# One queue, eight positions: reordering the transfers of steps 15 to 17 in a fused attention and MLP kernel

## The chip, the cores and the metric

The kernel runs on one core of one Trainium2 chip. The metric is the device time of one execution in microseconds; a figure for a kernel is the median over several executions. The profile is that of one execution, and its times count from the start of the profiled span.

## The reference

Two layers follow each other. The first is a decayed linear attention over 4 batches, 8 heads, 768 positions and 64 channels per head, in blocks of 64 positions with a state carried from block to block:

```
for each block b of 64 positions:
    intra = ((qb @ kb^T) * Dmask) @ vb
    inter = (qb * lam_pow) @ kv_state
    out   = intra + inter
    kv_state = lam_block * kv_state + (kb * rev_pow)^T @ vb
```

The second takes the attention output as a 3072 x 512 matrix x and computes `gelu_tanh(x @ w_in) @ w_out`, with an inner width of 2048. All inputs and the output are float32; the matmuls run in float16 with float32 sums.

## The kernel before

**Steps and groups.** The attention is cut into 24 steps, numbered 0 to 23. A step is 256 positions of one batch for four of the eight heads. Two steps make a superblock of 256 rows of x; the superblocks are put together into seven groups (line 533: `[[0, 1], [2], [3], [4, 5], [6, 7], [8, 9], [10, 11]]`), and each group runs the second layer on its rows. The matmuls of a group are cut into pieces that are put into a list, `filler`; `fill(n)` takes n pieces from it. So TensorE alternates between short bursts of attention and long runs of second-layer matmuls.

**The order of the work is written out by hand.** Every instruction is issued through `pin`, which keeps it in program order on its engine. Lines 913 to 1111 are the schedule. Nothing reorders it. What an engine waits for is decided by the data and by the rotation of buffers.

**One step, from load to score.** For step s the queries, keys and values are loaded by `load_step` (line 70) into float32 tiles of 256 KB each, which rotate over four buffers for each name. `cast_q` (line 282, on VectorE) multiplies the queries by their decay, `cast_k` (line 295, on ScalarE) converts the keys, both into one float16 tile. From step 8 on, `transpose_dma` (line 303) sends that tile through a transposing DMA into `qkT`, which rotates over five buffers. `scale_v` (line 266, on GpSimd) multiplies the values by the inverse decay.

**A burst.** Steps 13 to 16 and 18 to 23 are done two at a time by `burst(ns, ss)` (line 415): first `scores` of both steps in `ns` (line 350, into the PSUM tiles S), then, for the steps `ss` of the burst before, the products with the values (line 436) and with the carried state (line 461) into O, and the new state products K (line 450). In between the call may issue `ahead`, which for the burst of 15 and 16 is the preparation of step 17. Behind the matmuls come the masks of the scores on VectorE (line 360, `PT`), the copies of O into x on ScalarE (line 487), and the state updates (line 506 on VectorE, line 513 on GpSimd). A burst takes all eight PSUM banks: four S, two O, two K. The next second-layer matmul (line 560, `Hps`) goes into the bank of the first S, and so it waits until line 360 has read that one.

**The queue that the change is about.** All loads but two, all transposing DMAs and all stores are issued by SyncE, one after the other in program order. SyncE waits for what a transfer needs before it issues it, and whatever stands behind it waits too. The stores of a one-superblock group are issued by `store` inside `product` (line 662) at the moment when the piece that makes their data is taken from `filler`; for the third group (g = 2, rows 768 to 1023) there are two stores of 256 KB, one filled by VectorE at line 674 and one by ScalarE at line 656 and GpSimd at line 683.

**The order on that queue around the change.** The loop of steps 8 to 12 ends with n = 12, at lines 1032 to 1046. Written out, SyncE issues: transposition of 14; values of 15; values of 16; the two stores of the third group; transposition of 15; transposition of 16 (`prep_qk(16)`, line 1051); queries, keys, values of 17 (line 1052); queries, keys, values of 18 (line 1059); transposition of 17.

The lines of the schedule that matter:

```
1032        elif n == 12:
1033            load_step(15, "v")
1034            load_step(16, "v")
...
1044        if n == 12:
1045            prep_qk(15)
...
1051    prep_qk(16)
1052    load_ahead(17)
...
1055    burst((13, 14), (12,))
...
1061    burst((15, 16), (13, 14), ahead=lambda: (prep_qk(17), scale_v(17)))
```

Of the kernel before, what the change touches and what calls it, by code (L numbers as in the profile page):

```python
# [15 lines left out]
def kernel(  # L16
# [10 lines left out]
    nc = tc.nc  # L27
    pin = tc.keep_in_program_order
# [31 lines left out]
    def load_step(s, names="qkv"):  # L60
        b, r = divmod(s, 2 * NSB)
        sb, half = divmod(r, 2)
        ts = ld32.setdefault(s, [])
        for nm, src in (("q", q), ("k", k), ("v", v)):
            if nm not in names:
                continue
            t = ld.tile([P, HH, 2, D], FP32, tag=nm + "32", name=f"{nm}32_{s}")
            rows = src[b, half * HH : (half + 1) * HH, sb * SB : (sb + 1) * SB, :]
            queue = nc.scalar if (nm, s) == ("v", 0) else nc.sync
            pin(queue.dma_start(out=t[:].rearrange("p h j d -> p h (j d)"),  # L70
                                in_=rows.rearrange("h (p j) d -> p h (j d)", j=2)))
            ts.append(t)
# [97 lines left out]
    def load_ahead(s):  # L170
        if s < NSTEP:
            load_step(s)
# [76 lines left out]
    def wide(t):  # L249
        return t.rearrange("p j h d -> p h j d")  # L250

    def decay(t, s):
        hs = halves[s % 2]
        return t[:, hs, :].unsqueeze(3).to_broadcast([P, HH, 2, D])
# [9 lines left out]
    def scale_v(s):  # L264
        tv = a16p.tile([P, 2, HH, D], FP16, tag="v16", name=f"v16_{s}")
        pin(nc.gpsimd.tensor_tensor(wide(tv[:]), ld32[s][2][:], decay(dv, s), ALU.mult))  # L266
        a16[s] = a16[s] + (tv,)

    def prep_qk(s):
        cast_qk(s)  # L270
        transpose_dma(s)

    def cast_qk(s):
        cast_q(s)
        cast_k(s)

    def cast_q(s):
        q32 = ld32[s][0]
        tqk = a16p.tile([P, 2, 2, HH, D], FP16, tag="qk16", name=f"qk16_{s}")
        tq, tk = tqk[:, 0], tqk[:, 1]  # L280
        q_eng = nc.gpsimd if s == 3 else nc.vector
        pin(q_eng.tensor_tensor(wide(tq), q32[:], decay(dq, s), ALU.mult))  # L282
        if s == 0:
            inverse(halves[0])
            odd(halves[1])
            inverse(halves[1])
        a16[s] = (tq, tk)
        whole_qk[s] = tqk

    def cast_k(s):  # L290
        tk, k32 = a16[s][1], ld32[s][1]
        if s == 4:
            pin(nc.vector.tensor_copy(out=wide(tk), in_=k32[:]))
        else:
            pin(nc.scalar.activation(out=wide(tk), in_=k32[:], func=AF.Copy))  # L295
# [3 lines left out]
    def transpose_dma(s):  # L299
        tqk = whole_qk.pop(s)  # L300
        if s >= FIRST_DMA_T:
            o = qkp.tile([P, 2, 2, 2, P], FP16, tag="qkT", name=f"qkT_{s}")
            pin(nc.sync.dma_start_transpose(out=o[:].rearrange("p a j h t -> p (a j h) t"),
                                            in_=tqk[:].rearrange("p a j h d -> p (a j h d)")))
            qkT[s] = o
            if s == FIRST_DMA_T + 1:
                load_step(s + 1, "v")
# [225 lines left out]
    groups = [[0, 1], [2], [3], [4, 5], [6, 7], [8, 9], [10, 11]]  # L533
    group_of = {sb: (g, i) for g, sbs in enumerate(groups) for i, sb in enumerate(sbs)}
    filler = []
    o_pairs = {}

    def store_pair(pair):
# [4 lines left out]
    def queue_group(g, lead=0, per_set=0):  # L543
# [71 lines left out]
        def product(m, p, part=None):  # L615

            st = of_group

            def bank(name):
                if name not in st:  # L620
                    st[name] = ps_M.tile([P, 1 if name == "X" else NP, HE], FP32, tag="M",
                                         name="M" + name[0])
                return st[name]

            if m in (2, 5, 3):
                dst = bank("Y" if m in (5, 3) else "W")[:, p]
            else:
                dst = bank(f"X{p}")[:, 0]
            opens = m == 1 or (m in (2, 5) and p == 0)
            closes = m in (2, 3, 4)  # L630
            a, b = FACTORS[m]
            for i in range(HF) if part is None else range(HF // 2 * part, HF // 2 * part + HF // 2):
                lhsT = g_rows(a, i)[:, p * P : p * P + P]
                if b in W_SUMS:
                    rhs = w_sum16[:, w_slot[b], i, :]
                else:
                    F, E = b
                    rhs = w_out16[:, F * HF + i, E * HE : E * HE + HE]
                pin(nc.tensor.matmul(dst, lhsT, rhs, start=(opens and i == 0),  # L639
                                     stop=(closes and i == HF - 1), skip_group_check=True))  # L640
            if part == 0:
                return
            last = p == NP - 1

            def temp(name):
                if name not in st:
                    st[name] = mtp.tile([P, NP, HE], FP32, tag=name, name=name)
                return st[name]

            def out_tile(T):  # L650
                if f"o{T}" not in st:
                    st[f"o{T}"] = otp.tile([P, NP, 2, HE], FP32, tag="o32", name=f"o{T}")
                return st[f"o{T}"]

            def copy(to, of):
                pin(nc.scalar.activation(out=to, in_=of, func=AF.Copy))  # L656

            def store(T, ps=slice(0, NP), es=slice(0, 2)):
                r = row0 + T * HN
                rows = out[r : r + HN, :].rearrange("(p q) (e d) -> q p e d", q=P, e=2)  # L660
                for i in [slice(i, i + 1) for i in range(ps.start, ps.stop)]:
                    pin(nc.sync.dma_start(out=rows[:, i, es], in_=out_tile(T)[:, i, es, :]))

            one = slice(p, p + 1)
            if m == 1:
                copy(temp("m1")[:, p], dst)
            elif m == 2 and last:
                pin(nc.vector.tensor_tensor(out_tile(0)[:, :, 0, :], st["W"][:], st["m1"][:], ALU.add))
            elif m == 5 and last:
                copy(temp("q")[:], st["Y"][:])  # L670
            elif m == 6:
                copy(temp("u2")[:, p], dst)
            elif m == 3 and last:
                pin(nc.vector.tensor_tensor(out_tile(0)[:, :, 1, :], st["Y"][:], st["u2"][:], ALU.add))
                store(0)
            elif m == 7 and last_group:
                pin(nc.vector.tensor_tensor(out_tile(1)[:, p, 1, :], dst, st["q"][:, p], ALU.add))
                if last:
                    store(1, one, slice(1, 2))
            elif m == 7:  # L680
                copy(temp("u3")[:, p], dst)
                if last:
                    pin(nc.gpsimd.tensor_tensor(out_tile(1)[:, :, 1, :], st["u3"][:], st["q"][:],  # L683
                                                ALU.add))
            elif m == 4:
                copy(out_tile(1)[:, p, 0, :], dst)
                if last_group:
                    store(1, one, slice(0, 1 if last else 2))
                elif last:
                    store(1)  # L690
# [218 lines left out]
    def U(n):  # L909
        update(n, 1)  # L910
# [98 lines left out]
    for n, (a, b, c, d) in FILL.items():  # L1009
        stage_t(n)  # L1010
        fill(a + (n == 10))
        if n == 8:
            cast_q(n + 2)
            fill(1)
            cast_k(n + 2)
            transpose_dma(n + 2)
        else:
            prep_qk(n + 2)
        if n < 11:
            load_step(n + 4, "qkv" if n < 10 else "qk")  # L1020
        if n == 9:
            store_pair(1)
        if n == 11:
            scale_v(13)
            load_step(14, "v")
            load_step(16, "qk")
        elif n == 9:
            scale_v(11)
        elif n == 10:
            scale_v(12)  # L1030
            load_step(15, "qk")
        elif n == 12:
            load_step(15, "v")
            load_step(16, "v")
            scale_v(14)
        fill(b + (n == 8) - (n == 10))
        R(n, n - 1, keep=n == 8)
        fill(c)
        if n == 8:
            update(n, 0)  # L1040
            scale_v(n + 2)
            fill(2)
        U(n)
        if n == 12:
            prep_qk(15)
            scale_v(15)
        fill(d)
        if n > 8:
            sum_win((n - 7) // 2, (n - 1) % 2, nc.vector)

    prep_qk(16)
    load_ahead(17)
    scale_v(16)
    fill(3)
    burst((13, 14), (12,))
# [84 lines left out]
```

## Time and profile before

| what | value |
|---|---|
| device time, median of three executions | 200.13 us (199.81 to 200.23) |
| the profiled execution | 200.43 us, of which the span is 198.5 us |
| TensorE clock granted over the span | full |
| TensorE matmuls busy | 191.1 us, 96% of the span |
| VectorE busy | 152.5 us, 77% |
| ScalarE busy | 121.9 us, 61% |
| GpSimd busy | 73.0 us, 37% |
| moved by DMA | 38.13 MB, of which 37.50 MB on SyncE's queue |

How to read it. An engine's busy share says how much of the span it worked, not whether its idle time matters. For that one looks at the waits of the engine that sets the end, at the chain of work that ended last, and at the timeline of the stretch concerned. For a transfer two times count: when SyncE issued it, and when it landed. An issue row of the timeline shows only the first; from issue to landing a 256 KB load took 5.0 to 5.3 us in the middle of the page's issue table, and a store 4.6 us. A row such as `DMA_TRANSPOSE ... x2` merges two neighbours into one.

### The profile page before, as it was taken

The page shows a single profiled execution, that of the slowest core. Times are in us where ns is not written, and L with a number is a line of the kernel's source. Part 1 is how long each engine was busy: PE and PEld are TensorE (multiplying, and loading weights), DVE is VectorE, ACT ScalarE, POOL GpSimd, SP SyncE. Part 2 cuts the span into 40 slices and gives each one's busy share as a digit, 9 for nine tenths or more (in the row PEclk, how much of TensorE's full clock was granted, in tenths as well). Part 3 has the DMA queues.
Part 4 walks back from the last instruction along what each step waited for, and adds up shares of the span by engine and source line. Part 5 has one row for each costly group of instructions (what it writes and reads, how often), then busy time and mean ns, then how long its engine had stood idle before and what let it go on. Part 6 is the DMA issues. An engine that isn't in the chain of part 4 may idle for free.

```text
span 198.5 us, 5914 instructions
## 1 busy us (share of the span) xinstructions
PE 191.1 (96%) x2431; PEld 139.8 (70%) x2431; DVE 152.5 (77%) x297; ACT 121.9 (61%) x249; POOL 73.0 (37%) x85
## 2 busy tenths in 40 slices
PE   8979999999999999999799999999999999999993
PEld 2546544556888888654488855578888888888882
DVE  4897722889999889757899957998778996588620
ACT  3673878367874685677645377854768836779321
POOL 6594213466455831196372626256002030002000
PEclk9999999999999999999999999999999999999999
DMA  6999999999999999998995999410211300020205
GB/s 172 291 326 386 385 386 386 290 292 284 242 222 246 258 325 239 214 293 216 216 276 127 235 338 201 108 23 0 53 58 51 107 7 0 0 109 0 106 15 200
DMA packets 62810, 38.13 MB, mean 192 GB/s; under 512 B 18624, under 2 KB 55744, under 8 KB 62784
## 3 DMA queue, kind: packets, MB, share of 16 engines
q1 hardware_dynamic: 62240, 37.50, 73.5%
q8 instruction: 19, 0.31, 0.7%
q10 hardware_dynamic: 544, 0.26, 0.5%
q14 instruction: 7, 0.06, 0.1%
HBM read 27.26 MB, written 6.29 MB: 169 GB/s over the span
## 4 chain that ended last, share of the span: by engine, by line
PE 85%; DMA 7%; SPq 4%; ACT 1%; DVE 1%; issue 0%
PE Hps L560 22%; PE MX L639 18%; PE MY L639 9%; PE HX L730 7%; PE O2ps L575 7%; PE MW L639 4%; DMA wi<-in_moe_w_in_dram 4%; SPq L70 4%; PE HY L730 4%; PE S L350 3%; PE Hps L821 3%; DMA q<-in_q_dram 2%; PE HW L730 2%; PE OK L408 2%; PE OK L399 1%; PE O L461 1%
## 5 line engine op out<-in xcount | busy, mean ns | idle before, releaser
L560 PE MATMUL Hps<-xT,w_in 128*128 128x512 f16 (+1 forms) x288 | 50.5, 332 | 1.1 <-DVE PT L360 1.1
L513 POOL TENSOR_TENSOR u<-t,lumask 128x256 f16<-128x256 f32 x40 | 30.4, 776 | 41.6 <-DVE t L506 26.5
L560 PEld LDWEIGHTS <-w_in 128*128 128x128 f16 x288 | 27.9, 98 | 20.3 <-issue 1.3
L564 ACT ACTIVATE gT<-Hps 128x512 f16<-128x512 f32 x56 | 33.4, 598 | 11.6 <-PE Hps L560 11.1
L360 DVE TENSOR_TENSOR PT<-S,mask 128x512 f16<-128x512 f32 x48 | 30.3, 681 | 6.5 <-PE S L350 6.5
L266 POOL TENSOR_TENSOR v<-v,dv 128x512 f16<-128x512 f32 x24 | 27.9, 1165 | 18.2 <-DMA v<-in_v_dram 17.8
L639 PEld LDWEIGHTS <-gs 128*128 128x128 f16 x320 | 31.2, 98 | 3.6
L639 PEld LDWEIGHTS <-gT 128*128 128x128 f16 x240 | 23.3, 98 | 3.2 <-ACT gT L564 0.2
L282 DVE TENSOR_TENSOR qk<-q,dq 128x512 f16<-128x512 f32 x23 | 19.5, 851 | 3.2 <-DMA q<-in_q_dram 3.1
L639 PE MATMUL MX<-w_sum,gs 128*128 128x256 f16 x160 | 21.4, 273 | 0.0
L295 ACT ACTIVATE qk<-k 128x512 f16<-128x512 f32 x23 | 14.4, 625 | 9.5 <-DMA k<-in_k_dram 9.2
L683 POOL TENSOR_TENSOR o<-u,q 128x512 f32<-128x512 f32 (+1 forms) x5 | 6.0, 1205 | 34.9 <-ACT u L656 34.9
L609 DVE TENSOR_TENSOR gs<-gT 128x1024 f16<-128x1024 f16 (+1 forms) x24 | 16.0, 671 | 1.6 <-ACT gT L564 1.6
L575 PE MATMUL O2ps<-w_out,gT 128*128 128x512 f16 x64 | 14.6, 379 | 0.0
L487 ACT ACTIVATE xT<-OK 128x256 f16<-128x256 f32 x26 | 9.9, 452 | 6.5 <-PE OK L408 6.2
L730 PEld LDWEIGHTS <-ws 128*128 128x128 f16 x128 | 12.5, 97 | 1.8
L656 ACT ACTIVATE u<-MX 128x256 f32<-128x256 f32 x18 | 6.9, 383 | 10.2 <-PE MX L639 10.2
L609 DVE TENSOR_TENSOR gs<-gT,gs 128x1024 f16<-128x1024 f16 (+1 forms) x12 | 10.8, 901 | 0.3
L487 ACT ACTIVATE xT<-O 128x256 f16<-128x256 f32 x22 | 8.0, 459 | 4.9 <-PE O L461 4.0
L350 PEld LDWEIGHTS <-qkT 64*64 64x64 f16 x384 | 6.0, 106 | 6.8 <-issue 3.2
L575 PEld LDWEIGHTS <-gT 128*128 128x128 f16 x64 | 6.1, 98 | 6.6
L639 PE MATMUL MY<-w_out,gs 128*128 128x256 f16 x80 | 10.7, 272 | 0.0
(96 smaller groups left out, 316.7 us busy)
## 6 DMA issues: line engine op xcount, KB each, us to landing
q<-in_q_dram SPq DMA_DIRECT2D x24, 256.0 KB, 5.0
k<-in_k_dram SPq DMA_DIRECT2D x24, 256.0 KB, 5.1
v<-in_v_dram SPq DMA_DIRECT2D x23, 256.0 KB, 5.3
out_dram<-o SPq DMA_DIRECT2D x23, 256.0 KB, 4.6
wo<-in_moe_w_out_dram SPq DMA_DIRECT2D x4, 1024.0 KB, 9.5
wi<-in_moe_w_in_dram SPq DMA_DIRECT2D x4, 512.0 KB, 8.2
wi<-in_moe_w_in_dram SPq DMA_DIRECT2D x2, 1024.0 KB, 12.8
v<-in_v_dram ACTq DMA_DIRECT2D x1, 256.0 KB, 4.3
```

What stands on the lines that cost most here:

```text
L266: pin(nc.gpsimd.tensor_tensor(wide(tv[:]), ld32[s][2][:], decay(dv, s), ALU.mult))
L282: pin(q_eng.tensor_tensor(wide(tq), q32[:], decay(dq, s), ALU.mult))
L295: pin(nc.scalar.activation(out=wide(tk), in_=k32[:], func=AF.Copy))
L360: pin(nc.vector.tensor_tensor(t[:, hl].rearrange("p b c d -> p b (c d)"), Sps[:].rearrange("p b c d -> p b (c d)"), mask[:].unsqueeze(1).t ...
L487: pin(nc.scalar.activation(out=d, in_=o, func=AF.Copy))
L513: pin(nc.gpsimd.tensor_tensor(u[:], state[half][:].unsqueeze(2).to_broadcast([P, 2, 2, D]), lumask[:, 2 * half : 2 * half + 2, :].unsqueez ...
L560: pin(nc.tensor.matmul(by_block(Hps[:, i, :]), w_in16[:, c, f * P : (f + 1) * P], x(c), start=(c == 0), stop=(c == NC - 1)))
L564: pin(nc.scalar.activation(out=dst, in_=Hps[:], func=AF.Gelu_apprx_tanh))
L575: pin(nc.tensor.matmul(O2[tau][0][:], gT[:, f % HF, f // HF, tau * P : (tau + 1) * P], w_out16[:, f, :], start=(n == 0), stop=(n == NF - 1)))
L609: pin(nc.vector.tensor_tensor(g_rows(m, i), g_rows(a, i), g_rows(b, i), op))
L639: pin(nc.tensor.matmul(dst, lhsT, rhs, start=(opens and i == 0), stop=(closes and i == HF - 1), skip_group_check=True))
L730: pin(nc.tensor.matmul(dst[:, i, :], w_in_block(a, slice(c, c + 1), slice(f * P, f * P + P))[:, 0], x_block(b, slice(c, c + 1))[:, 0], sta ...
```

## The change

Three moves on SyncE's queue, and nothing else: no instruction is added or taken away, and the order on the four compute engines is that of before.

1. The transposition of 15 stands right behind that of 14. The loads of the values of 15 and 16 move behind it.
2. The queries and keys of 17 stand ahead of the transposition of 16; the values of 17 stay behind it. To that end `prep_qk(16)` is written out as its two halves, the casts and the transposition.
3. The two stores of the third group are kept in a list, `kept_stores`, when their data is made, and are issued behind the values of 17.

The aim is that transfers which a later step waits for are not held up on the queue by those that nobody waits for. The new order is: transpositions of 14 and 15; values of 15; values of 16; queries and keys of 17; transposition of 16; values of 17; the two stores; queries, keys, values of 18; transposition of 17.

```
+    kept_stores = []
...
             def store(T, ps=slice(0, NP), es=slice(0, 2)):
                 r = row0 + T * HN
                 rows = out[r : r + HN, :].rearrange("(p q) (e d) -> q p e d", q=P, e=2)
-                for i in [slice(i, i + 1) for i in range(ps.start, ps.stop)]:
-                    pin(nc.sync.dma_start(out=rows[:, i, es], in_=out_tile(T)[:, i, es, :]))
+                o = out_tile(T)
+
+                def send():
+                    for i in [slice(i, i + 1) for i in range(ps.start, ps.stop)]:
+                        pin(nc.sync.dma_start(out=rows[:, i, es], in_=o[:, i, es, :]))
+
+                if g == 2:
+                    kept_stores.append(send)
+                else:
+                    send()
...
         elif n == 12:
-            load_step(15, "v")
-            load_step(16, "v")
             scale_v(14)
...
         if n == 12:
             prep_qk(15)
+            load_step(15, "v")
+            load_step(16, "v")
             scale_v(15)
...
-    prep_qk(16)
-    load_ahead(17)
+    cast_qk(16)
+    load_step(17, "qk")
+    transpose_dma(16)
+    load_step(17, "v")
+    while kept_stores:
+        kept_stores.pop(0)()
     scale_v(16)
```

## Prediction

> **What bounds the kernel now.** I read the page first, then TensorE's waits, then the chain of work that ended last, then the timelines of the stretch that these point to. Part 1 of the page, with busy us, share of the span and number of instructions:
>
> ```profile
> PE 191.1 (96%) x2431; PEld 139.8 (70%) x2431; DVE 152.5 (77%) x297; ACT 121.9 (61%) x249; POOL 73.0 (37%) x85
> ```
>
> TensorE is busy for 96% of the span, so only what makes it idle can change the end. Its waits between 40 us and 198 us, as us in total, times, longest:
>
> ```profile
> PE Hps L560 <- DVE PT L360: 1.1, 1, 1.1
> ```
>
> That is one single wait in 158 us. TensorE's own timeline around it shows where it lies:
>
> ```profile
> 93.68 0.64 PE L350 MATMUL S<-qkT 64*64 64x128 f16 x32
> ...
> 94.95 0.51 PE L461 MATMUL O<-qkT,u 128*128 128x128 f16 x6
> 96.59 1.67 PE L560 MATMUL Hps<-xT,w_in 128*128 128x512 f16 x7 [1.13 <-DVE PT L360]
> ```
>
> The burst of steps 15 and 16 begins at 93.68 and ends at 94.95 + 0.51 = 95.46; then TensorE stands still for 1.13 us until 96.59. The chain of work that ended last says why (start, us, what):
>
> ```profile
> 90.08 0.19 SPq L303
> 90.26 0.05 issue
> 90.32 4.91 DMA q<-in_q_dram
> 95.22 0.02 issue
> 95.25 0.69 DVE qk L282
> 95.94 0.61 DVE PT L360
> 96.55 0.04 issue
> 96.59 3.61 PE Hps L560 x16
> ```
>
> Read upward: the matmul waits for a bank that the first mask (line 360) must have read; the mask stands behind the query cast of step 17 (line 282) on VectorE; the cast waits until the queries of 17 have landed at 95.22; they were issued at 90.32, as soon as SyncE was through with a transposition. SyncE's timeline tells what held it up:
>
> ```profile
> 81.47 1.72 SPq L303 DMA_TRANSPOSE qkT<-qk  x1
> 83.24 1.13 SPq L70 DMA_DIRECT2D v<-in_v_dram  x2
> 84.47 1.78 SPq L662 DMA_DIRECT2D out_dram<-o  x2
> 86.42 3.84 SPq L303 DMA_TRANSPOSE qkT<-qk  x2
> 90.32 0.57 SPq L70 DMA_DIRECT2D q<-in_q_dram  x1
> ```
>
> In order: transposition of 14, values of 15 and 16, two stores, transpositions of 15 and 16, queries of 17. The stores take 1.78 us because the second starts only at 85.90, when GpSimd has finished its output tile at 85.87. The cast tile of 15 was complete at 83.23 (VectorE 82.55 + 0.68, ScalarE 82.36 + 0.62), so its transposition stood ready for 3.2 us behind others.
>
> [...] the wait of the second store to 85.87 holds the transposition of 15 until 86.42. [...] Here the queries of 17 had arrived on 12 of 16 engines by 93.49, and on the last at 95.22. [...] the scores of 15 began at 93.68, yet their mask began at 95.86, behind the cast. [...] So I use landing times for arrivals.
>
> **The change part by part.** The counts and orders on the four compute engines stay; only SyncE's order moves. What SyncE will do, from 83.19 on, when it has issued the transposition of 14:
>
> *Transposition of 15 forward.* Ready at 83.23. An issue takes, over the 16 of before, as ns min/median/max and as us to landing:
>
> ```profile
> L303 SPq DMA_TRANSPOSE qkT<-qk x16: 1233/1510/3418, 50.7 to 141.0; - x16
> DMA to landing us min/median/max: 3.0/4.6/6.4
> ```
>
> I take 1.8 (it stands right behind another, whose data moves only from about 84.4 to 85.4), so it is issued by 85.0; the ends are 84.5 and 86.7. It lands near 87.5 instead of 91.40. Nobody gains from that by itself: its scores begin at 93.68.
>
> *Values of 15 and 16 back by one transposition.* Issued at 85.0 and 85.6 instead of 83.24 and 83.92, landing at 88 to 89.5 and 89 to 90.5 instead of 86.87 and 87.82 (3.6 and 3.9 us of before, up to 5). GpSimd's two multiplications (1.05 us each) then end by about 91.6, at worst 92.6, instead of 89.08. Queued behind them on GpSimd are the four state tiles of line 513, 0.61, 0.61, 1.06, 1.06 us. The burst at 93.68 reads the values at about 94.55 and the first two of the state tiles at 94.95; they are there by 92.8, at worst 93.8. Cost: nothing, hidden behind TensorE's second-layer matmuls.
>
> *Queries and keys of 17 forward.* Issued at about 86.1 and 86.7 instead of 90.32 and 90.93. At 4.9 us to landing the queries arrive at 91.0; the ends are 89.3 (3.2 us, the quickest load of this stretch, at 98.15) and 93.0 (6.9 us, the queries of 15). VectorE is free at 93.13, so the cast runs from 93.13 to 93.82 without a wait. In the burst before, the first mask began 0.46 us after the scores (87.62 against 87.16); so here at 94.14, ending at 94.83. The bank is free at about 94.88, and TensorE needs it at 95.46. The wait of 1.13 us goes away whole, with 0.6 us to spare. The keys land by 93.5 at worst; ScalarE casts them behind the gelu that ends at 94.39, ahead of the first copy of O at about 95.2.
>
> *Transposition of 16 behind three more transfers.* Its tile is complete at 85.79. It is issued at about 87.3 instead of 88.95 and lands 4.6 us later at 91.9, at most 6.4 later at 93.7, instead of 92.22. TensorE needs it about 0.28 us into the burst, at 93.96. On the expected path nothing is lost, but this is the thinnest margin of the change.
>
> *Values of 17 and the stores.* The values go out near 89.5 (91.51 before), and are multiplied on GpSimd after the state tiles, for a step that begins at 104.5. The stores go out near 90 instead of 84.47; the output pool has three buffers, and the buffer that waits for the first of these stores is written next at 112.6. Cost nothing. The loads of 18 follow at about 91 (92.06 before), the transposition of 17 no later than before.
>
> *Sum:* 1.13 us from TensorE's path, nothing added. Behind 96.59 TensorE has no wait over 0.06 us to the end, so the shift carries through if the others keep up. VectorE, busy without pause from 95.25 to 115.80, starts that stretch 1.7 us earlier (first mask 94.14 instead of 95.86), more than TensorE's 1.13. 200.13 - 1.13 = 199.0.
>
> **The rivals.** *Only a part is gained.* The profiled execution took 200.43 us, the others 199.81 to 200.23; if the wait is shorter without the profile, the gain is too. And if a transposition stalls the DMA engines, as from 88.75 to 90.25, where they moved 60 GB/s against 347 before and 265 after, the transposition of 16 comes up to 1.5 us later than 91.9 plus some lag, 94.5, and TensorE waits 0.5 there. Gain about 0.6: 199.5.
>
> *The wait is not there in undisturbed executions.* For: a single DMA engine brought the queries 1.7 us after the 12 others, and with 93.49 as landing there would have been no wait. Against: the keys and values of 17 and 18 trail alike, so it is no chance of one packet. Then 200.1.
>
> *Slower: the transposition of 16 becomes the bound.* With the longest issue (3.4 us) for that of 15, SyncE reaches that of 16 at 88.9; 6.4 us to landing is 95.3, and a stall of 1.5 us on top 96.8. The burst's remaining 1.5 us of matmuls follows, so the next second-layer matmul begins at 96.8 to 98.3 instead of 96.59: 0.2 to 1.7 us lost, 200.9 in the middle. For: that longest issue stood beside an equally full queue at 76.12. Against: two more transfers stood ahead then, and total data ahead of the transposition of 16 is what it was, two stores traded for two loads.
>
> **How the numbers follow.** Full gain 0.64 (199.0), part 0.14 (199.5), none 0.10 (200.1), slower 0.12 (200.9). The predicted time is the likeliest, 199.0. The range from 198.6 (the scatter of 0.4 below) to 200.3 holds the first three cases and a little of the last. Faster by over 0.2%, that is below 199.73: 0.78; within: 0.10; slower: 0.12.
>
> **What would show it.** Right: SyncE issues the queries of 17 near 86 and they land before 93.1; line 282 shows no wait for them; the first mask begins near 94.1; TensorE's waits from 40 us on are empty. The step on the transposition of 16 is wrong if the scores of 16 wait for line 303; the step on the values if line 450 or 461 waits for GpSimd. The whole is wrong if TensorE loses the 1.13 us again behind 96 us, at a bank or a gelu sum.

## The result and the profile after

The changed kernel takes 198.91 us (median of six executions, 198.90 to 198.94) against 199.78 us of the kernel before (six executions beside it, 199.24 to 200.23). The ratio is 0.9957, with a 95% interval of 0.994 to 0.9974: faster by 0.4%. The forecast was 199.0. An execution more than 1.5% above the fastest of its kernel counts as slow and is left out of all medians and ratios; that was one each in four of the variants below.

The profiled spans are 198.5 us before and 197.1 us after. Part 1 of the page after:

```profile
PE 191.5 (97%) x2431; PEld 140.0 (71%) x2431; DVE 151.6 (77%) x297; ACT 122.2 (62%) x249; POOL 73.3 (37%) x85
```

The same work in a span that is 1.4 us shorter. TensorE's waits from 40 us to 198 us, as in the prediction; no line stands under the heading, since no wait is left:

```profile
core 0 of [0], span 197.1 us
engine line waited for: us in total, times, longest us
```

TensorE's timeline over the burst of 15 and 16 (start, us, instruction):

```profile
93.60 0.64 PE L350 MATMUL S<-qkT 64*64 64x128 f16 x32
...
94.86 0.51 PE L461 MATMUL O<-qkT,u 128*128 128x128 f16 x6
95.21 2.10 PE L561 MATMUL Hps<-xT,w_in 128*128 128x512 f16 x9
```

The burst begins 0.08 us earlier than before (93.60 against 93.68), and the second-layer matmul behind it follows at once, at 95.21 instead of 96.59. That is 1.38 us, the whole difference of the spans: from this matmul to the end it is 101.9 us in both profiles. The chain of work that ended last is now TensorE alone through this stretch:

```profile
93.67 0.57 PE S L350 x32
94.24 0.45 PE O L436 x32
94.68 0.25 PE K L450 x24
94.93 0.44 PE O L461 x6
95.37 3.45 PE Hps L561 x16
```

No transfer and no VectorE instruction stands between the burst and the second layer any more. SyncE's timeline, in the new order, tells why:

```profile
81.81 3.33 SPq L303 DMA_TRANSPOSE qkT<-qk  x2
85.19 1.24 SPq L70 DMA_DIRECT2D v<-in_v_dram  x2
86.47 1.55 SPq L70 DMA_DIRECT2D q<-in_q_dram  x1
88.07 0.51 SPq L70 DMA_DIRECT2D k<-in_k_dram  x1
88.73 1.40 SPq L303 DMA_TRANSPOSE qkT<-qk  x1
90.24 0.52 SPq L70 DMA_DIRECT2D v<-in_v_dram  x1
90.80 1.01 SPq L666 DMA_DIRECT2D out_dram<-o  x2
```

The queries of 17 go out at 86.47 instead of 90.32 and land 4.6 us later, at 91.09 instead of 95.22. VectorE's timeline takes them up without a wait:

```profile
93.09 1.10 DVE L282 TENSOR_TENSOR qk<-q,dq 128x512 f16<-128x512 f32 x1
94.10 2.47 DVE L360 TENSOR_TENSOR PT<-S,mask 128x512 f16<-128x512 f32 x4
```

And the transpositions' issues, ns min/median/max, and us to landing:

```profile
L303 SPq DMA_TRANSPOSE qkT<-qk x16: 1233/1688/3422, 50.7 to 139.6; - x16
...
DMA to landing us min/median/max: 3.0/5.1/6.6
```

They became no cheaper: the median issue is 1688 ns instead of 1510. The gain is in what stands behind what.

### The profile page after: what moved, and what is told of

Same layout as the page of the kernel before. It is cut to its first block, busy times and chain, and to the rows that moved or that the text cites. A ratio compares the mean times of both kernels' runs of the same rounds, so it can differ in the third digit from the quotient of the medians.

```text
span 197.1 us, 5915 instructions
## 1 busy us (share of the span) xinstructions
PE 191.5 (97%) x2431; PEld 140.0 (71%) x2431; DVE 151.6 (77%) x297; ACT 122.2 (62%) x249; POOL 73.3 (37%) x85
## 4 chain that ended last, share of the span: by engine, by line
PE 89%; SPq 4%; DMA 4%; ACT 0%; issue 0%
PE Hps L561 25%; PE MX L640 18%; PE MY L640 9%; PE HX L739 7%; PE O2ps L576 7%; PE MW L640 4%; DMA wi<-in_moe_w_in_dram 4%; SPq L70 4%; PE HY L739 4%; PE S L350 3%; PE Hps L830 3%; PE HW L739 2%; PE OK L408 2%; PE O L461 1%; PE O L436 1%; PE OK L399 1%
## 5 line engine op out<-in xcount | busy, mean ns | idle before, releaser
L513 POOL TENSOR_TENSOR u<-t,lumask 128x256 f16<-128x256 f32 x40 | 30.9, 787 | 39.5 <-DVE t L506 25.8
L282 DVE TENSOR_TENSOR qk<-q,dq 128x512 f16<-128x512 f32 x23 | 18.4, 802 | 1.7 <-DMA q<-in_q_dram 1.7
L610 DVE TENSOR_TENSOR gs<-gT 128x1024 f16<-128x1024 f16 (+1 forms) x24 | 16.9, 711 | 1.6 <-ACT gT L565 1.6
L640 PE MATMUL MX<-w_sum,gT 128*128 128x256 f16 x80 | 10.4, 273 | 0.0
```

The lines of the kernel that those rows point to most:

```text
L513: pin(nc.gpsimd.tensor_tensor(u[:], state[half][:].unsqueeze(2).to_broadcast([P, 2, 2, D]), lumask[:, 2 * half : 2 * half + 2, :].unsqueez ...
L610: pin(nc.vector.tensor_tensor(g_rows(m, i), g_rows(a, i), g_rows(b, i), op))
```

## The experiments

One theory and its rivals. The theory: TensorE's one wait is as long as the queries of 17 land late, because their cast stands ahead of the first mask on VectorE; any edit that makes them land early enough, or takes the cast out of the mask's way, gives all of the gain, as long as nothing else comes late. The rivals: it is the place of one certain transfer (the transposition of 15, or the queries ahead of the transposition of 16), or the transfers become faster in themselves, or the wait belongs to the profiled execution only. All times below are medians of executions beside the kernel before on the same chip; the ratios are worked out from all of these executions and are not exactly those of the medians.

### The third part alone: the stores behind the values of 17

```
     prep_qk(16)
     load_ahead(17)
+    while kept_stores:
+        kept_stores.pop(0)()
```

with `store` as in the change.

> Third part alone: the two stores of the third group go behind the values of 17; transposition of 15 still behind the values of 15 and 16, queries of 17 still behind the transposition of 16. Theory (TensorE's one wait is as long as the queries of 17 are late, landing minus about 94.1): without the 1.8 us of the stores SyncE issues the queries near 88 instead of 90.3, they land near 93, the wait is 0 to 0.3 us, and the time is 198.9 to 199.2. Rival (it is the early transposition of 15, or the queries standing ahead of the transposition of 16, that counts): time as before, 199.8, wait near 1.1.

Measured: 199.13 us against 199.59, ratio 0.9976 (0.9962 to 0.9991). In its profile TensorE has no wait from 40 us on and the span is 197.1. SyncE's timeline, with both transpositions and then the queries:

```profile
84.17 3.79 SPq L303 DMA_TRANSPOSE qkT<-qk  x2
88.01 0.82 SPq L70 DMA_DIRECT2D q<-in_q_dram  x1
```

The queries go out at 88.01, where the theory had put them, and land at 91.87. So the stores alone were enough in this execution. The timed ones scatter from 198.86 to 200.13, much more than those of the full change: not every execution gains all. (Three of the 22 have spans of 197.9 to 198.1 us, the others 196.9 to 197.4.)

### The second part alone: queries and keys of 17 ahead of the transposition of 16

```
-    prep_qk(16)
-    load_ahead(17)
+    cast_qk(16)
+    load_step(17, "qk")
+    transpose_dma(16)
+    load_step(17, "v")
```

> Second part alone: queries and keys of 17 ahead of the transposition of 16, stores and transposition of 15 where they were. Theory: the queries are issued near 88.8 and land near 93.7, so the wait behind line 282 is gone; the transposition of 16 is issued near 90 and lands between 93.3 and 94.8, where the scores of 16 need it at 93.96, so up to 0.8 us may be lost there; time 198.9 to 199.7. Rival (the stores alone are the cause): time as before, 199.8.

Measured: 199.97 us against 199.59, ratio 1.0014 (0.9994 to 1.0034); no gain, where 198.9 to 199.7 was expected, and executions from 198.96 to 200.64. TensorE's timeline:

```profile
93.59 0.42 PE L350 MATMUL S<-qkT 64*64 64x128 f16 x16
94.91 0.42 PE L350 MATMUL S<-qkT 64*64 64x128 f16 x16 [0.90 <-DMA qkT<-qk]
...
96.30 1.89 PE L560 MATMUL Hps<-xT,w_in 128*128 128x512 f16 x8
```

The queries landed at 92.33 and the wait behind the cast is gone, but the scores of 16 now wait 0.90 us for the transposition of 16, a little over the upper end of what was expected. One wait was traded for another. That is the risk that the prediction named. The third part is what keeps it away, as the combinations below show: parts 2 and 3 together have no wait, parts 1 and 2 have a longer one.

### The queue untouched, the cast behind the masks

```
         for i, n in enumerate(ns):
             scores(n)
-            if ahead and i == 0:
-                ahead()
...
         for n in ns:
             causal(n)
+        if ahead:
+            ahead()
```

> The queue exactly as before; instead the preparation of 17 is issued behind the four masks of the burst of 15 and 16, so that the first mask does not stand behind the cast that waits for the queries. Theory: the queries land as late as before, near 95, but nothing on TensorE's path waits for them; first mask near 94.1, no wait of TensorE, time 198.9. Rival (the gain comes from the transfers themselves: earlier transpositions, fewer stalls of the DMA engines): time as before, 199.8.

Measured: 199.11 us against 199.59, ratio 0.9979 (0.9969 to 0.9989); span 197.1, no wait of TensorE from 40 us on. The queries landed at 94.59; by the estimate of landing minus about 94.1, from the profile of before, TensorE would have waited some 0.5 us for a mask behind the cast. First VectorE's timeline, then TensorE's:

```profile
94.06 2.48 DVE L360 TENSOR_TENSOR PT<-S,mask 128x512 f16<-128x512 f32 x4 [1.07 <-PE S L350]
96.45 0.68 DVE L282 TENSOR_TENSOR qk<-q,dq 128x512 f16<-128x512 f32 x1
```

```profile
94.86 0.51 PE L459 MATMUL O<-qkT,u 128*128 128x128 f16 x6
95.21 2.54 PE L560 MATMUL Hps<-xT,w_in 128*128 128x512 f16 x11
```

The masks start as soon as the scores are there, and the second layer starts at 95.21, to the hundredth where the changed kernel has it. SyncE's order was not touched. This shows the middle of the chain: the queries mattered only because VectorE took their cast first. The time is 0.2 us above the 198.9 that was expected, but no wait is left over there. The span of every execution is on record: its mean over the 22 is 197.22 us, against 197.18 over the nine of the changed kernel below. The difference lies outside the span: device time less span is 1.96 us on average here, 1.94 in the kernel before beside it, and 1.81 in the changed kernel. What that is isn't shown.

### Two loads more ahead of the queries

```
     prep_qk(16)
+    load_step(18, "qk")
     load_ahead(17)
...
-    load_ahead(18)
+    load_step(18, "v")
```

> Kernel of before with the queries and keys of 18 issued ahead of those of 17: two loads more in front of the queries of 17. Theory: they land two landings (0.87 us each) later, near 97, and TensorE's wait grows by the same 1.7 us to about 2.9; time about 201.5. Rival (the wait at the first mask is only what the profile shows, and in executions without it the queries come in time): growth of clearly less than 1.7 us, 199.8 to 200.6.

Measured: 201.12 us against 199.59, ratio 1.0103 (1.0059 to 1.0148). Between the medians that is 1.53 us more, where 1.7 was expected; the ratio also takes in an execution of 203.72 us, which had a lower clock (see the last section). The rival that the wait exists in the profiled execution only falls: every execution is at least 1.1 us above the median of before. TensorE's timeline:

```profile
94.97 0.51 PE L461 MATMUL O<-qkT,u 128*128 128x128 f16 x6
97.18 2.10 PE L560 MATMUL Hps<-xT,w_in 128*128 128x512 f16 x9 [1.70 <-DVE PT L360]
```

In this profile the queries landed at 95.81, only 0.6 us later than in that of before, and the wait is 0.57 us longer. The expected landing near 97 and wait of 2.9 were missed, because they were counted from a profile with one late DMA engine. The trace has sixteen landing times for the queries, one for each engine that carried a share. In the profile of before fifteen shares had landed by 94.10 and the last at 95.22; here it is 95.75 and 95.81. So the fifteenth engine came 1.65 us later, which is close to the 1.7 of two landings. The relation between landing and wait holds.

### The kernel before, profiled once more

No edit.

> The kernel of before, profiled once more. Theory: the span moves with TensorE's one wait, and the wait with the landing of the queries of 17: wait = landing minus about 94.1, span = 197.1 plus the wait within 0.2. Rival (the scatter of before comes from elsewhere): the span differs from that by more.

Measured: 199.76 us against 199.72, ratio 1.0005 (0.9988 to 1.0023). TensorE's timeline:

```profile
96.32 2.97 PE L560 MATMUL Hps<-xT,w_in 128*128 128x512 f16 x13 [0.91 <-DVE PT L360]
```

Three profiles with the same instructions at this place can be set side by side:

| kernel | queries landed | wait | landed minus wait | span |
|---|---|---|---|---|
| before, again | 94.96 | 0.91 | 94.05 | 198.2 |
| before | 95.22 | 1.13 | 94.09 | 198.5 |
| two loads more | 95.81 | 1.70 | 94.11 | 199.1 |

The wait follows the landing to within 0.06 us. The spans are 197.1 plus the wait plus 0.2 to 0.3: for the first that is just inside the 0.2 that was expected, for the other two a little outside. A good part of it is that the wait, counted from the end of the last burst matmul, understates the lost time: that matmul lasts 0.22 us, while in the changed kernel the next one starts 0.06 us after its start. In the profile of before that start came 1.35 us after it.

### The other combinations of the three parts

The first part alone leaves the stores ahead of both transpositions:

```
         elif n == 12:
-            load_step(15, "v")
-            load_step(16, "v")
             scale_v(14)
...
             prep_qk(15)
+            load_step(15, "v")
+            load_step(16, "v")
```

> First part alone: the stores now stand directly behind the transposition of 14, and the transposition of 15, the values of 15 and 16, the transposition of 16 and the queries of 17 all behind them. Theory: the transposition of 16 lands at 94 to 95.5 and the queries at 96.3, some 1.1 us later than before, so TensorE waits about 2.2 us in all; 200.5 to 201.5. Rival (bringing the transposition of 15 forward helps by itself): 199.8 or less.

Measured: 201.02 us against 199.72, ratio 1.0062 (1.0041 to 1.0083). TensorE's timeline has both waits, 1.67 us together, where 2.2 was expected; the queries landed at 95.46, not at 96.3:

```profile
94.65 0.42 PE L350 MATMUL S<-qkT 64*64 64x128 f16 x16 [0.62 <-DMA qkT<-qk]
...
97.25 1.02 PE L560 MATMUL Hps<-xT,w_in 128*128 128x512 f16 x4 [1.05 <-DVE PT L360]
```

The first and second part without the third:

```
         elif n == 12:
-            load_step(15, "v")
-            load_step(16, "v")
             scale_v(14)
...
             prep_qk(15)
+            load_step(15, "v")
+            load_step(16, "v")
...
-    prep_qk(16)
-    load_ahead(17)
+    cast_qk(16)
+    load_step(17, "qk")
+    transpose_dma(16)
+    load_step(17, "v")
```

> First and second part without the third: the two stores stand directly behind the transposition of 14 and ahead of everything else. Theory: the second store still waits for GpSimd until 85.9, so the transposition of 15 goes out at 86.4, the values of 15 and 16 near 88 and 88.5, the queries near 89, the transposition of 16 near 90.3. The queries land in time, but the transposition of 16 lands near 95 against a need at 93.96, and the values of 16 reach line 450 and the state tiles line 461 1 to 2 us late; TensorE waits there, 200 to 201.5. Rival (only the landing of the queries counts): 198.9.

Measured: 204.18 us against 199.77, ratio 1.0209 (1.017 to 1.0249), worse than expected. TensorE's timeline:

```profile
97.17 0.42 PE L350 MATMUL S<-qkT 64*64 64x128 f16 x16 [3.15 <-DMA qkT<-qk]
```

The second store started only at 86.16. The transposition of 16 was issued at 90.99, took 2.7 us to issue and let the scores of 16 begin at 97.17; a landing near 95 was expected. The queries, which were expected in time, landed at 95.39. What they and the values would have cost is hidden behind the wait of 3.15. This profiled execution took 202.44 us; the wait explains that one, but not the 204.18 of the median (see the last section).

The first and third part without the second, with `store` as in the change:

```
         elif n == 12:
-            load_step(15, "v")
-            load_step(16, "v")
             scale_v(14)
...
             prep_qk(15)
+            load_step(15, "v")
+            load_step(16, "v")
...
     prep_qk(16)
     load_ahead(17)
+    while kept_stores:
+        kept_stores.pop(0)()
```

> First and third part without the second: transposition of 15 behind that of 14, values of 15 and 16, transposition of 16, then queries, keys, values of 17 and the stores. Theory: the queries are issued near 88.4 and land at 92.3 to 93.3, still by 93.13 or a little over, so no wait or one of some 0.1 us: 198.9 to 199.1; the second part is then not needed beside the other two. Rival (the queries ahead of the transposition are what makes the gain): 199.5 or more.

Measured: 198.91 us against 199.77, ratio 0.9951 (0.9932 to 0.9971). The queries landed at 91.94, the transposition of 16 at 91.00; no wait.

The second and third part without the first, with `store` as in the change:

```
-    prep_qk(16)
-    load_ahead(17)
+    cast_qk(16)
+    load_step(17, "qk")
+    transpose_dma(16)
+    load_step(17, "v")
+    while kept_stores:
+        kept_stores.pop(0)()
```

> Second and third part without the first: the transposition of 15 stays behind the values of 15 and 16. Theory (the stores are what mattered, and with them gone either place of the transposition of 15 does): queries issued near 86.5, landed near 91; transposition of 16 landed by 93; no wait of TensorE; 198.9 to 199.1. Rival (the transposition of 15 must go first): a wait at the scores, 199.5 or more.

Measured: 199.01 us against 199.72, ratio 0.9969 (0.9957 to 0.9982). No wait; queries at 91.00, transposition of 16 at 92.67.

And the whole change again, with no further edit:

> The changed kernel once more, beside the variants below. Theory (before scatters because the landing of the queries of 17 does, and the changed kernel has slack for it): 198.9, and a scatter much narrower than the 2 us of before. Rival (scatter of the chip): as wide as before.

Measured: 198.93 us (198.79 to 199.61, nine executions) against 199.77 (199.17 to 201.09, thirty), ratio 0.9949 (0.9925 to 0.9972).

| parts of the change | us | ratio to before |
|---|---|---|
| 1 | 201.02 | 1.0062 |
| 2 | 199.97 | 1.0014 |
| 3 | 199.13 | 0.9976 |
| 1, 2 | 204.18 | 1.0209 |
| 1, 3 | 198.91 | 0.9951 |
| 2, 3 | 199.01 | 0.9969 |
| 1, 2, 3 | 198.93 | 0.9949 |

All with the third part gain, all without it don't. Without the third part, the first puts more transfers behind the store that waits for GpSimd (with parts 1 and 2 the second store started at 86.16), and the second sends the transposition of 16 later. Beside the third part, the first one seems to bring the rest of the gain (199.13 to 198.91, with intervals that still overlap). Only about half of these 0.22 us lie in the span (197.27 on average for part 3, 197.16 for parts 1 and 3); the rest lies outside it (1.93 against 1.79), for which no cause is shown. The second part adds nothing that can be measured.

### The thinnest margin

```
     load_step(17, "qk")
-    transpose_dma(16)
     load_step(17, "v")
     while kept_stores:
         kept_stores.pop(0)()
+    transpose_dma(16)
```

> The changed kernel with the transposition of 16 behind the values of 17 and the stores too, three transfers later. In the changed kernel it landed at 93.09, and its scores need it at about 93.9. Theory (that is the thinnest margin, 0.8 us): it lands near 95.7, the scores of 16 wait 1.7 us for it, time about 200.6. Rival (margin is wide, other work fills in): 198.9 to 199.2.

Measured: 200.89 us against 199.77, ratio 1.0064 (1.0041 to 1.0088). The transposition of 16 landed at 96.12. TensorE's timeline:

```profile
93.58 0.42 PE L350 MATMUL S<-qkT 64*64 64x128 f16 x16
96.17 0.42 PE L350 MATMUL S<-qkT 64*64 64x128 f16 x16 [2.17 <-DMA qkT<-qk]
```

The wait is 2.17 us where the changed kernel has none. The margin is real, and of the size that was read from the profile after: three transfers later is 3.0 us later, and the scores wait all of it but 0.86.

### Both cures at once

The edit of `burst` from above, on the changed kernel:

```
-            if ahead and i == 0:
-                ahead()
...
         for n in ns:
             causal(n)
+        if ahead:
+            ahead()
```

> The changed kernel with the preparation of 17 behind the masks as well, that is both cures of the one wait. Theory (there is one wait, and it is cured): nothing more to gain, 198.9 within 0.1. Rival (each cures something of its own): 198.5 or less.

Measured: 198.98 us against 199.72, ratio 0.9956 (0.9938 to 0.9974). Nothing on top: both cure the same wait, and there is no second one. None of the variants beats the changed kernel.

## Why the prediction was right

**The wait and its chain.** Bank, mask, cast, queries, queue: each link was predicted from one view. The links from the queue to the mask were shown by experiments. Without the stores ahead of them the queries land in time (91.87, no wait); with the cast behind the masks their landing is of no account (94.59, no wait); with two loads more the loss grows (95.81, a wait of 1.70 us). The rival that the wait exists in the profiled execution only fell with the last of these. The link from the mask to the bank was not cut by itself; it is read from the traces, where line 360 ends the wait of line 560 in all three profiles of the table.

**The queue's times.** The transposition of 15 was to be issued by 85.0 and was at 85.14; the queries were to go out at 86.1 and land at 91.0, and did at 86.47 and 91.09; the first mask was to begin at 94.14, and did at 94.10. The values of 15 and 16 landed at 89.39 and 90.25, inside the stated span, and GpSimd was through with them at 91.59, as worked out; they cost nothing. (The burst of 15 and 16 reads them itself: its state products K, line 450, are those of its own steps, not of the burst before.) The stores and the later loads cost nothing either.

**Terms that were mis-sized, without changing the outcome.** The transposition of 15 landed at 88.69, not at 87.5. The transposition of 16 landed at 93.09 (92.53 in the second profile), not at 91.9: the issue of the queries took SyncE 1.55 us, not the 0.57 of before, so the transposition went out at 88.73 instead of 87.3. Of the two us that the prediction saw as margin, 0.8 remained. The cast took 1.10 us instead of 0.69, with GpSimd at work beside it, and used up the gap ahead of the first mask; with some 0.4 us more TensorE would have waited, by an estimate: the first mask began at 94.10 and took 0.68 us, and TensorE wrote to its bank from 95.21 on. The wait was worth 1.30 us in the profile, not 1.13, by the starts of the matmuls. And one sum of the prediction is off: 0.2 to 1.7 us lost on 200.13 has its middle at 201.1, not at 200.9.

**The size of the gain, and luck.** 1.13 us were predicted from the one profile of before. Between the medians it was 0.87, between the full gain and the first rival, by which the wait is shorter in other executions. The profile of before was of an execution that took 200.43 us, longer than all six timed beside it, and all of its wait hung on one late DMA engine: with the fifteenth, at 94.10 instead of 95.22, the relation of the table gives no wait. In the second profile of before the fifteenth came at 94.72 and the last at 94.96. What held the one engine up isn't shown.

The spans of the executions tell the same. The thirty of before beside the last run of the changed kernel have a mean span of 197.91 us, from 197.2, where little or no wait can be left, to 199.1. The nine of the changed kernel have 197.18. So 0.73 us of the gain lie in the span, where the wait is. Some 0.15 more lie outside it (device time less span: 1.96 before, 1.81 after); the prediction has no term for them, and no run explains them.

That 199.0 was met within 0.1 us is in part luck. The wait of a late execution, 0.26 us more than the gain between the medians, was taken from a median of three executions that was 0.35 us above that of the six.

That the whole scatter of before comes from the wait isn't shown. The changed kernel, which has slack there, lost most of it: 198.79 to 199.61 against 199.17 to 201.09.

## What to carry to other kernels

On a kernel that keeps one engine busy for 96%, look for the single wait that remains and follow it back to the transfer; then ask what stands ahead of that transfer on its queue that nobody waits for. A store that waits for its data is the first suspect: in the profile of before the second store started only at 85.90, when its data was there, and the transposition behind it at 86.42. Moving the urgent transfers ahead without moving that store made things worse here (201.02 us with part 1 and 204.18 with parts 1 and 2, against 199.72 and 199.77). Before moving one up, read how much slack each transfer has that moves down: here the transposition of 16 had 0.8 us left, and spending it cost more than the change had gained (200.89 us against 199.77 of before). And size the gain from several executions: the two profiles of before show waits of 1.13 and 0.91 us, and the medians differ by 0.87.

## What the runs showed of the hardware

**In one profile the clock fell after a wait.** In the profile with the transposition of 16 behind the stores, TensorE waited 2.17 us, but the span is 201.1, 4.0 us over that of the changed kernel. The busy times in stretches of 2 us (us, PE busy, PEld, DVE, ACT, POOL, granted clock, DMA share, GB/s) show the rest:

```profile
94.00:96.00 2.00, 0.00 (x1) 0.00 (x0) 1.30 (x3) 0.81 (x2) 2.00 (x3) 1.00 1.25 155
96.00:98.00 2.00, 1.83 (x79) 1.61 (x80) 1.14 (x2) 0.30 (x1) 0.06 (x1) 0.85 1.23 291
98.00:100.00 2.00, 2.00 (x6) 0.76 (x5) 2.00 (x7) 1.46 (x5) 1.39 (x2) 0.50 1.22 301
100.00:102.00 2.00, 2.00 (x9) 0.79 (x7) 1.17 (x3) 0.81 (x2) 0.99 (x3) 0.79 1.22 291
```

TensorE works again from 96.17 on. At 97.42 the granted clock fell to half for 3.41 us, and a 512-wide matmul started every 427 ns instead of every 216. By an estimate from these figures, 3.41 us at half speed lose 1.7 us, which with the wait makes 3.9 of the 4.0. The wait alone doesn't account for the lower clock: 2.17 us of idling came before it here, while the longer wait of 3.15 us in the profile of parts 1 and 2 passed at a granted clock of 1.00 in every stretch from 88 to 106. What lowered the clock isn't shown.

The mean clock of every execution is on record; in this profile, with one such stretch, it is 0.992. Of the five executions of parts 1 and 2, the profiled one had 1.000 and took 202.44 us; three had 0.992 and took 203.38 to 204.27; one had 0.981 and took 204.98. With two loads more, four at 0.999 or above took 200.75 to 201.40 us, and the one at 0.992 took 203.72. So a lower clock goes with a part of what these two variants lose, in some executions and not in others. Whether and where a stretch at half clock lay in them isn't shown, and four executions of other variants and of before had 0.991 and took only 199.48 to 200.64 us.

**The long casts stood beside a busy GpSimd.** VectorE made 322 casts of queries (line 282) in the fourteen profiles. The 122 during which GpSimd did nothing took 0.68 to 0.69 us. Every cast of more than 0.70 us, up to 1.76, had GpSimd at work during it. No run takes GpSimd away from one cast, so the cause isn't tested.
